# Turning all attention outputs back to features on VectorE instead of through DRAM

## The chip, the cores and the metric

One core of a Trainium2 chip runs the whole program. The metric is the time of one execution in microseconds of device time, as the median of several runs. An execution is also recorded by the hardware profiler; its span goes from the first to the last instruction, and its own time is about 2 us longer.

## The reference

Two attention blocks of width D = 640 with 32 heads of 20 features work on 2048 tokens each. Their outputs stand side by side in one result of 2048 x 1280 (bf16).

```python
# A: four segments of L = 512 tokens, causal inside a segment, plus a memory of the earlier ones
for s in range(4):
    p = softmax(qs @ ks.T * scale + causal_mask)
    a_dot = p @ vs
    a_mem = (phi(qs) @ M) / (phi(qs) @ z + 1e-6)        # phi(t) = t + 1 if t > 0 else exp(t)
    o = g * a_mem + (1 - g) * a_dot                     # g = sigmoid(beta), one per head
    M += phi(ks).T @ vs;  z += phi(ks).sum(tokens)
a = concat(o over segments, heads) @ wo_A
# B: causal attention with a window of 256 tokens
b = softmax(q @ k.T * scale + window_mask) @ v  -> heads side by side @ wo_B
out = concat([a, b], axis=-1)
```

## The kernel before

The work is cut into eight chunks of 512 tokens, alternating between the blocks: A0, B0, A1, B1, A2, B2, A3, B3, numbered n = 0 to 7. Two chunks overlap at any time, each in two halves of 16 heads. Heads are handled in eight groups g of four, one head to each 32 partitions.

For a chunk, these jobs run on the engines:

- `qk_job` (line 391) projects q and k on PE (`m` tiles, five matmuls of 128x512 each), copies them to `st`, and SP stores them to DRAM and loads them spread out (one head to 32 partitions; lines 351 and 368). `v_job` (565) projects v, and SP copies parts of it (lines 606, 618 to 621).
- `score_batch` (638) makes scores on PE into the `sc` banks of PSUM (lines 662 and 672). ACT takes their exponential into `pt` (line 682), GpSimd (POOL) masks most of them (728, 732), VectorE the half blocks (713).
- `one_group` (1270) sums p times v for a group (line 746), and for A also the memory part (`mem`, 754). The result stands as features x tokens in one PSUM bank. `turn` (763) transposes it in 32x32 blocks on VectorE into `tt` (line 769), so that tokens lie on partitions, and `norm` (773) divides by the sum (792, 787) and writes it to `o`. Where the second part of an A group comes, it is put in `u` and GpSimd adds it to `o` (804). After the turn, `o` has 32 tokens of each 32-row block on the partitions and, along the free axis, 16 blocks of tokens by 160 features of one of four head classes.
- The output projection needs features on partitions. For chunks 0 to 6, `final_job` (812) does this by DMA: four stores on SP write `o` to `scr_o` in DRAM with tokens as rows (line 818), and in `final_part` (836) a DMA transpose for each 256 tokens brings it back as `oT` (line 845), of which there are two buffers. Ten matmuls for each 128 tokens (line 857), in two halves of 320 columns, then two copies to `ot` on ACT or VectorE (lines 210 and 212), and a store to the output (870).
- For the last chunk, `back` (875) turns `o` once more on VectorE in 32x32 blocks, as soon as four groups of a 128-token tile are there, into a view of `qA`. `final_turned` (887) multiplies it with a second copy of `wo_B`, whose rows are in the order that these turns leave (`wo2`, loaded into `wk_A` by `load_wo2`, line 223).

All instructions are issued in an order that the program works out when it is built. `Flow` holds a clock for each engine, and each step adds a fixed duration to it. The main loop of `body` takes whatever is ready by those clocks: due DMAs, the next score batch, a pending group, a job, a job of `fins` (the output projections, last in the list). Work for VectorE goes in when its clock is behind PE's (`when_idle`, `flush`); where nothing is ready, PE gets a filling matmul (`fill`, line 993). The numbers of `ORDER` make small random choices between such steps at each score batch (`pick`). On the chip every engine works off its own queue strictly in order, and so does SP, which issues nearly all DMAs. There are two PSUM banks (`m0`, `m1`) for everything but scores; a bank is free again when VectorE or ACT has read it.

Of the kernel before, what the change touches and what calls it, by code (L numbers as in the profile page):

```python
# [28 lines left out]
    0, 57, 0, 852, 0, 771, 969, 354, 517, 150, 469, 627, 861, 162, 75, 0, 574, 779, 904, 517,  # L29
    524, 666, 803, 190, 0, 0, 953, 0, 405, 169, 677, 960, 622, 0, 392, 443, 517, 185, 61, 913,  # L30
    240, 994, 430, 0, 412, 385, 759, 595, 219, 521, 782, 621, 0, 804, 507, 481, 812, 481, 0,
    742, 0, 235, 388, 0, 591, 501, 847, 431, 349, 878, 434, 976, 36, 797, 549, 0, 0, 39, 668,
    959, 355, 121, 912, 0, 0, 768, 0, 679, 0, 0, 560, 924, 137, 985, 626, 0, 720, 957, 332,
    336, 390, 7, 0, 531, 661, 678, 0, 733, 400, 415, 975, 582, 0, 146, 814, 370, 94, 515, 0,
    678, 823, 209, 259, 781, 0, 814, 18, 360, 301, 230, 0, 950, 0, 406, 599, 768, 275, 0, 820,
    0, 181, 865, 0, 619, 0, 48, 579, 0, 0, 854, 0, 713, 0, 421, 775, 330, 420, 719, 898, 0,
    303, 685, 986, 0, 479, 49, 97, 362, 991, 0,
# [4 lines left out]
NOT = 2  # L42
# [133 lines left out]
class _K:  # L176
# [45 lines left out]

    def load_wo2(self, w_ap):

        self.wo2 = self.wk_A
        yield "dma", self.f.pe + 9000.0
        self.nc.sync.dma_start(out=self.wk_A[:], in_=w_ap)
        self.f.on_dma(1, 2100.0)
# [544 lines left out]
    def norm(self, tt, dst, add, last):  # L773
# [21 lines left out]
        def s2():  # L795
            if not add:
                part(dst)
                last()
                return
            u = self.wk.tile([P, NB, DH], BF16, name="u", bufs=NU)  # L800
            t = part(u[:], self.u_free[-NU])

            def both():
                nc.gpsimd.tensor_tensor(out=dst, in0=dst, in1=u[:], op=ALU.add)
                self.u_free.append(f.on_pool(716.0, t + DVE_OUT) + POOL_OUT)
                last()
            f.at(t + DVE_OUT, both)
# [4 lines left out]
    def final_job(self, n, o, scr, wo, out2d, col, t0, t1):  # L812
        nc, f = self.nc, self.f
        t = max(f.dve, f.pool) if n % 2 == 0 else f.dve
        yield "dma", t
        a, b = t0 * P, min(t1 * P, self.toks[n])
        for j in range(4):
            nc.sync.dma_start(
                out=scr[a:b, GW * j:GW * (j + 1)].rearrange("(b t) c -> t b c", t=HD),
                in_=o[HD * j:HD * (j + 1), a // HD:b // HD, :])  # L820
        t = f.on_dma(4, 1.76 * (b - a), t)
        yield "dma", t - 200.0
        for x0 in range(a, b, 256):
            yield from self.final_part(n, scr, wo, out2d, col, x0, min(b, x0 + 256), t)
        if t1 * P >= self.toks[n]:
            self.mark(f.pe, "fin", n)

# [8 lines left out]
    def final_part(self, n, scr, wo, out2d, col, a, b, t):  # L836
        nc, f = self.nc, self.f
        free = lambda: None if self.ot_n - NOT not in self.ot_done else 0.0
        while free() is None or self.urgent:
            yield "dma", free  # L840
            yield "dma", self.calm
        mine = self.ot_n
        self.ot_n += 1
        oT = self.big.tile([P, self.KT, 256], BF16, name="oT", bufs=NOT)
        nc.sync.dma_start_transpose(out=oT[:, :, 0:b - a], in_=scr[a:b, :])
        yield f.on_dma(1, 100.0, t, 950.0 + 3.83 * (b - a), 2100.0) + 600.0
        for tt in range(a // P, (b + P - 1) // P):
# [3 lines left out]
            w = min(P, b - tt * P)  # L851
            x = tt * P - a
            for hf in range(2):
                yield "bank"
                ps, bi = self.bank()
                for m in range(self.KT):
                    nc.tensor.matmul(ps[0:w, 0:320], lhsT=oT[:, m, x:x + w],  # L857
                                     rhs=wo[:, m, 320 * hf:320 * hf + 320],
# [4 lines left out]
                t = self.evac(ot[0:w, 320 * hf:320 * hf + 320], ps[0:w, 0:320], 320, 408.0)  # L863
                self.close(bi, t)
                f.open = False
            r = self.row0[n] + tt * P
            lo = max(0, -r)

            def store(ot=ot, r=r, lo=lo, w=w, k=k):
                nc.sync.dma_start(out=out2d[r + lo:r + w, col:col + self.D], in_=ot[lo:w, :])  # L870
                self.ot_free[k] = f.on_dma(1, 400.0, t + DVE_OUT)
            f.at(t + 300.0, store)
        self.ot_done.add(mine)

    def back(self, o, qt, g0):

        if g0 == 0:
            self.oD[qt] = self.qA[:].rearrange("p g s -> p (g s)")[
                :, self.D * qt:self.D * (qt + 1)].rearrange(
                "p (c b t) -> p c b t", c=LT + 1, b=LT)  # L880
        a, b = (0, 2) if g0 == 0 else (2, LT + 1)
        self.nc.vector.transpose(
            out=self.oD[qt][:, a:b, :, :].rearrange("p c b t -> p b c t"),
            in_=o[:, LT * qt:LT * qt + LT, :].rearrange("p b (c r) -> p b c r", r=HD)[:, :, a:b, :])
        self.f.on_dve(60.0 + 1.05 * P * (b - a))

    def final_turned(self, out2d, r, col, qt):
        nc, f = self.nc, self.f
        oD = self.oD[qt]
        end = qt == LT - 1  # L890
        yield f.dve + DVE_OUT
        yield from self.ot_wait()
        k = len(self.ot_free) - 1
        ot = self.wk.tile([P, 640], BF16, name="ot", bufs=3)
        for hf in range(2):
            yield "bank"
            ps, bi = self.bank()
            cs = slice(320 * hf, 320 * hf + 320)
            for m in range(self.KT):
                nc.tensor.matmul(ps[:, 0:320], lhsT=oD[:, m, :, :].rearrange("p b t -> p (b t)"),  # L900
                                 rhs=self.wo2[:, m, cs],
                                 start=(m == 0), stop=(m == self.KT - 1))
                f.on_pe("full", mm_ns(320))
                if m < self.KT - 1:
                    yield 0.0
            t = self.evac(ot[:, cs], ps[:, 0:320], 320, 408.0)
            self.close(bi, t)
            f.open = False
            if end:
                (nc.scalar if hf == 0 else nc.sync).dma_start(  # L910
                    out=out2d[r:r + P, col + 320 * hf:col + 320 * hf + 320], in_=ot[:, cs])

        def store():
            nc.sync.dma_start(out=out2d[r:r + P, col:col + self.D], in_=ot[:])
            self.ot_free[k] = f.on_dma(1, 400.0)
        if end:
            self.ot_free[k] = f.pe + 3000.0
        else:
            f.at(t + 300.0, store)
# [423 lines left out]
def laid_out(A_x, A_wq, A_wk, A_wv, A_wo, A_beta, B_x, B_wqkv, B_wo):  # L1343
# [18 lines left out]
    def heads(w):  # L1362
        return w.reshape(G, 4, DH, D).transpose(1, 0, 2, 3).reshape(D, D)
# [37 lines left out]
```

## Time and profile before

| what | us |
|---|---|
| median of 5 runs (lowest, highest) | 372.06 (369.36, 373.47) |
| time of the profiled execution | 368.91 |
| its span | 366.8 |
| TensorE matmuls busy | 331.6 |
| ScalarE busy | 318.6 |
| VectorE busy | 273.5 |
| GpSimd busy | 154.3 |

The mean granted TensorE clock was 0.986 of full speed. The DMA engines moved 61.12 MB. In the lists below, a line of a group has the source line, the engine, the operation, what it writes and reads with shapes, the count, the busy time with the mean duration of one in ns, and the idle time of the engine before it with what ended it. Busy times of groups are larger than the engine's share, as neighbours in a queue overlap by some tens of ns. A timeline line has the start, the length, the engine and line, and in square brackets the idle time before it.

### The profile page before, as it was taken

How to read it: one execution, taken by the hardware profiler on the slowest of the kernel's cores; microseconds unless marked ns; L12 is line 12 of the kernel's file. 1: busy time of each engine (PE TensorE's matmuls, PEld its weight loads, DVE VectorE, ACT ScalarE, POOL GpSimd, SP SyncE). 2: the span in 40 equal slices, each digit the busy share in tenths (PEclk: the TensorE clock that was granted, in tenths of full speed). 3: DMA queues.
4: the chain of work that ended last, by engine and by line, in shares of the span. 5: the costliest groups of instructions: out<-in, count | busy, mean ns of one | idle time of the engine just before them, and what ended most of it. 6: DMA issues, size and time to landing. Idle time of an engine off the chain costs nothing.

```text
span 366.8 us, 17742 instructions
## 1 busy us (share of the span) xinstructions
PE 331.6 (90%) x7670; PEld 185.4 (51%) x7720; DVE 273.5 (75%) x557; ACT 318.6 (87%) x412; POOL 154.3 (42%) x241
## 2 busy tenths in 40 slices
PE   8899997997989889999998699997999998997887
PEld 3445553553544544654545345553555555564554
DVE  7556884585898779988897598985888597885540
ACT  2877992997999999999999799997999899987844
POOL 8211230341345436643726365554537436365310
PEclk9999998999999999999999999997899999999999
DMA  7995574666794764567365843468333874278442
GB/s 233 410 395 149 160 169 124 166 123 179 180 278 127 157 154 125 139 179 216 118 190 157 170 112 115 128 177 205 105 117 105 216 210 124 73 154 187 121 117 100
DMA packets 85430, 61.12 MB, mean 167 GB/s; under 512 B 46056, under 2 KB 83304, under 8 KB 85352
## 3 DMA queue, kind: packets, MB, share of 16 engines
q1 hardware_dynamic: 84776, 59.57, 59.6%
q8 instruction: 60, 0.98, 1.2%
q10 hardware_dynamic: 576, 0.42, 0.4%
q14 instruction: 18, 0.15, 0.1%
HBM read 25.73 MB, written 23.72 MB: 135 GB/s over the span
## 4 chain that ended last, share of the span: by engine, by line
PE 41%; DMA 18%; ACT 16%; DVE 11%; issue 8%; SPq 4%; POOL 1%; ACTq 0%; DVEq 0%; POOLq 0%
ACT pt L682 15%; PE m L408 11%; PE m L746 7%; PE m L857 6%; PE sc L672 5%; PE m L578 4%; SPq L368 3%; PE sc L662 3%; DVE tt L769 2%; DMA pqA<-scr_pq 2%; DVE pt L713 2%; DMA wv_A<-in_A_wv_dram 2%; DMA pkT<-scr_pk 2%; DMA beta<-in_A_beta_dram 1%; DVE o L787 1%
## 5 line engine op out<-in xcount | busy, mean ns | idle before, releaser
L682 ACT ACTIVATE pt<-sc 128x1024 bf16<-128x1024 f32 (+1 forms) x328 | 283.5, 973 | 18.6 <-PE sc L672 11.8
L732 POOL TENSOR_SCALAR_AFFINE_SELECT pt<-pt 128x512 bf16<-128x512 bf16 x128 | 90.1, 704 | 161.9 <-ACT pt L682 149.1
L769 DVE STREAM_TRANSPOSE tt<-m 128x512 f32<-128x512 f32 x88 | 62.1, 711 | 30.4 <-PE m L746 28.4
L212 DVE CAST st<-m 128x512 bf16<-128x512 f32 x60 | 40.9, 681 | 16.3 <-PE m L408 13.0
L728 POOL TENSOR_SCALAR_AFFINE_SELECT pt<-pt 128x512 bf16<-128x512 bf16 x56 | 38.7, 692 | 33.4 <-ACT pt L682 33.4
L578 PEld LDWEIGHTS <-xT 128*128 128x128 bf16 x400 | 32.7, 99 | 17.3 <-issue 6.4
L787 DVE TENSOR_TENSOR o<-tt,rr 128x320 bf16<-128x320 f32 x64 | 34.7, 544 | 1.1
L857 PEld LDWEIGHTS <-oT 128*128 128x128 bf16 x280 | 24.7, 97 | 16.0 <-issue 4.6
L672 PE MATMUL sc<-qB,kB 32*128 32x64 bf16 (+3 forms) x896 | 30.2, 223 | 2.2 <-issue 1.3
L672 PE MATMUL sc<-qA,kA 32*128 32x64 bf16 (+3 forms) x640 | 29.1, 251 | 2.7 <-issue 2.0
L578 PE MATMUL m<-wv_A,xT 128*128 128x320 bf16 (+2 forms) x200 | 29.1, 285 | 2.2 <-DMA wv_A<-in_A_wv_dram 1.4
L578 PE MATMUL m<-wBv,xT 128*128 128x320 bf16 (+2 forms) x200 | 27.5, 273 | 0.7
L857 PE MATMUL m<-wo_A,oT 128*128 128x320 bf16 x160 | 26.8, 300 | 0.4 <-DVE ot L212 0.3
L408 PE MATMUL m<-xT,wBk 128*128 128x512 bf16 x83 | 24.4, 380 | 2.8 <-issue 1.4
L746 PE MATMUL m<-pt,vB 128*32 128x64 bf16 (+3 forms) x896 | 23.9, 225 | 2.7 <-ACT vB L210 1.0
L672 PEld LDWEIGHTS <-kB 32*128 32x128 bf16 x896 | 14.4, 93 | 23.2 <-issue 20.9
L408 PE MATMUL m<-xT,wBq 128*128 128x512 bf16 x89 | 24.4, 380 | 0.9 <-issue 0.3
L408 PE MATMUL m<-xT,wk_A 128*128 128x512 bf16 x78 | 22.2, 381 | 3.3 <-ACT st L210 2.2
L408 PE MATMUL m<-xT,wq_A 128*128 128x512 bf16 x82 | 23.2, 399 | 0.8 <-issue 0.2
L746 PE MATMUL m<-pt,vA 128*32 128x64 bf16 (+3 forms) x640 | 22.3, 257 | 1.4 <-ACT st L210 0.5
L857 PE MATMUL m<-wo_B,oT 128*128 128x320 bf16 x120 | 20.5, 300 | 3.2 <-ACT ot L210 1.5
L672 PEld LDWEIGHTS <-kA 32*128 32x128 bf16 x640 | 10.6, 92 | 25.4 <-issue 22.6
(99 smaller groups left out, 466.4 us busy)
## 6 DMA issues: line engine op xcount, KB each, us to landing
out_dram<-ot SPq DMA_DIRECT2D x31, 160.0 KB
scr_o<-o SPq DMA_DIRECT2D x28, 160.0 KB
scr_kB<-st SPq DMA_DIRECT2D x20, 128.0 KB
scr_qB<-st SPq DMA_DIRECT2D x20, 128.0 KB
kB<-scr_kB SPq DMA_DIRECT2D x32, 80.0 KB
qB<-scr_qB SPq DMA_DIRECT2D x32, 80.0 KB
scr_kA<-st SPq DMA_DIRECT2D x18, 128.0 KB
scr_qA<-st SPq DMA_DIRECT2D x18, 128.0 KB
```

The lines of the kernel that those rows point to most:

```text
L212: nc.vector.tensor_copy(out=out, in_=in_)
L368: self.nc.sync.dma_start(out=dst[HD * j:HD * j + DH, g0:g0 + 4, :], in_=rows.rearrange("(g j d) s -> j d g s", g=4, j=4)[j])
L408: nc.tensor.matmul(ps[:, :], lhsT=w_ap[:, kt, m * P:(m + 1) * P], rhs=xT[:, kt, :], start=(kt == 0), stop=(kt == self.KT - 1))
L578: nc.tensor.matmul(ps[:, c0:c0 + w], lhsT=xT[:, kt, tt * P:(tt + 1) * P], rhs=w_ap[:, kt, a:a + w], start=(kt == 0), stop=(kt == self.KT - 1))
L672: nc.tensor.matmul(ps[j // 2][:, j % 2, c0:c0 + 64 * nb], lhsT=k[rows, g, P * kc:P * kc + P], rhs=q[rows, g, 64 * b0:64 * (b0 + nb)], star ...
L682: nc.scalar.activation(out=pt[:, 2 * i:2 * i + 2, 0:hi], in_=ps[i][:, :, 0:hi], func=ACT.Exp, scale=self.scale)
L728: nc.gpsimd.affine_select(out=blk, in_=blk, pattern=[[0, r], [-1, w]], compare_op=ALU.is_ge, fill=self.zero, base=-1, channel_multiplier=1)
L732: nc.gpsimd.affine_select(out=blk, in_=blk, pattern=[[0, r], [1, w]], compare_op=ALU.is_ge, fill=self.zero, base=128 - w, channel_multipli ...
L746: nc.tensor.matmul(O[HD * j:HD * j + HD, c:c + 64 * nb], lhsT=self.vcols(v, h // 16 if vk[0] == "v" else 0, vt, h, HD), rhs=rhs[j], start= ...
L769: self.nc.vector.transpose(out=tt[:], in_=O[:, :])
L787: nc.vector.tensor_tensor(out=out, in0=a, in1=b, op=ALU.mult)
L857: nc.tensor.matmul(ps[0:w, 0:320], lhsT=oT[:, m, x:x + w], rhs=wo[:, m, 320 * hf:320 * hf + 320], start=(m == 0), stop=(m == self.KT - 1))
```

## The change

The way through DRAM goes for all chunks. A new job, `back_job`, is made with the first group of a chunk 0 to 6. It allocates `oD` (two buffers, 5 x 512 columns) and makes five transposes of 128x512 on VectorE, each as soon as the groups that its features come from are complete; it waits for the output projections of the chunk two before. The last chunk turns as before, in two pieces for each tile, into a buffer of `xT` in place of `qA`. Both kinds of chunk use one `final_job`, which takes `oD` as it is. `wo_A` and `wo_B` are laid out on the host in the order of rows that the turns leave, so the second copy of `wo_B` and its load go. `o` has two buffers in place of three, and a group of a chunk is only taken up once the chunk two before has been turned. Whether a part of a group is the first or is to be added is decided when its `norm` step is issued. `ORDER` has other numbers.

```diff
-    def load_wo2(self, w_ap):
...
-    def final_job(self, n, o, scr, wo, out2d, col, t0, t1):
...
-            nc.sync.dma_start(
-                out=scr[a:b, GW * j:GW * (j + 1)].rearrange("(b t) c -> t b c", t=HD),
-                in_=o[HD * j:HD * (j + 1), a // HD:b // HD, :])
...
-        nc.sync.dma_start_transpose(out=oT[:, :, 0:b - a], in_=scr[a:b, :])
...
+    def back(self, n, o, b0, nb, x, y):
+        self.nc.vector.transpose(
+            out=self.oD[n][:, x:y, b0:b0 + nb, :].rearrange("p c b t -> p b c t"),
+            in_=o[:, b0:b0 + nb, :].rearrange("p b (c r) -> p b c r", r=HD)[:, :, x:y, :])
+        self.f.on_dve(50.0 + 1.05 * HD * nb * (y - x))
+
+    def back_job(self, n, o):
+        f = self.f
+        if n >= 2:
+            yield self.known(n - 2, "out")
+        self.oD[n] = self.big.tile([P, self.KT, L // HD, HD], BF16, name="oD", bufs=2)
+        for c, last in enumerate((1, 3, 4, 6, 7)):
+            for g in range(0 if c == 0 else last, last + 1):
+                yield self.known(n, "o", g)
+            def go(c=c):
+                self.back(n, o, 0, L // HD, c, c + 1)
+                if c == self.KT - 1:
+                    self.mark(f.dve + DVE_OUT, n, "oD")
+            f.when_idle(f.pe, go, go)
+            yield f.pe + 1.0
+
+    def final_job(self, n, wo, out2d, col, qts):
...
+            yield self.known(n, "oD", qt) if n == len(self.chunks) - 1 else self.known(n, "oD")
...
-                    nc.tensor.matmul(ps[0:w, 0:320], lhsT=oT[:, m, x:x + w],
-                                     rhs=wo[:, m, 320 * hf:320 * hf + 320],
+                    nc.tensor.matmul(ps[:, 0:320], lhsT=oD[:, m, :, :].rearrange("p b t -> p (b t)"),
+                                     rhs=wo[:, m, cs],
...
-                    need = [max(p[4] for p in ps_) + 100.0, self.done.get((n, "v", g))]
+                    need = [max(p[4] for p in ps_) + 100.0, self.done.get((n, "v", g)),
+                            self.done.get((n - 2, "oD")) if n > 1 else 0.0]
...
-            o_t[n] = self.big.tile([P, L // HD, GW], BF16, name="o", bufs=3)
+            o_t[n] = self.big.tile([P, L // HD, GW], BF16, name="o", bufs=2)
+            if n < len(self.chunks) - 1:
+                self.jobs.append(self.job(self.back_job(n, o_t[n])))
+            else:
+                t = self.big.tile([P, self.KT, L], BF16, name="xT", bufs=2)
+                self.oD[n] = t[:].rearrange("p c (b t) -> p c b t", t=HD)
...
-        "A_wk": rows(A_wk), "A_wq": rows(A_wq), "A_wv": rows(A_wv), "A_wo": rows(heads(A_wo)),
+        "A_wk": rows(A_wk), "A_wq": rows(A_wq), "A_wv": rows(A_wv), "A_wo": turned(A_wo),
...
-        "B_wo": rows(heads(B_wo)), "B_wo2": turned(B_wo)}
+        "B_wo": turned(B_wo)}
```

## The prediction

> **What bounds the kernel now.** I read the page's first two parts, then the groups with shapes kept apart, the busy time of each engine in stages, and last the timelines of single engines where a stage is not full. The profiled execution took 368.91 us around a span of 366.8; the sum below is made against it. It lies 3.15 us under the median of the runs, 372.06, so the change found is then added to the median.
>
> ```profile
> PE 331.6 (90%) x7670; PEld 185.4 (51%) x7720; DVE 273.5 (75%) x557; ACT 318.6 (87%) x412; POOL 154.3 (42%) x241
> ```
>
> TensorE (PE) and ScalarE (ACT) are both nearly full, VectorE (DVE) is the third. 75% sounds like room, but it is an average. I cut the span at the half-block masks on VectorE (every third one), which stand in the same place in all queues before and after, and joined or split some stages. Columns: stretch, length, then busy time of PE, PEld, DVE, ACT, POOL.
>
> ```profile
> 116.80:143.90 27.10, 24.51 (x671) 13.10 (x676) 22.74 (x48) 25.50 (x33) 13.33 (x19) 1.00 0.59 137
> 143.90:175.00 31.10, 30.30 (x712) 17.30 (x719) 27.81 (x59) 30.92 (x39) 16.10 (x24) 1.00 0.62 177
> 175.00:206.80 31.80, 27.30 (x784) 16.27 (x782) 25.89 (x52) 30.45 (x37) 17.23 (x25) 1.00 0.61 157
> 206.80:234.80 28.00, 26.39 (x644) 13.79 (x640) 23.47 (x48) 26.80 (x33) 13.30 (x18) 1.00 0.44 119
> 330.90:347.20 16.30, 12.75 (x497) 8.15 (x496) 8.52 (x19) 12.72 (x18) 7.19 (x12) 1.00 0.68 151
> 347.20:366.85 19.65, 15.57 (x199) 10.52 (x182) 5.16 (x11) 9.09 (x19) 1.33 (x2) 1.00 0.38 113
> ```
>
> From 117 to 235 us PE is busy 92% of the time, ACT 96%, DVE 85%: no engine has much left. In the last 19.65 us no scores are made any more; PE works off output projections, and ACT and DVE are half idle or more. So the kernel ends late because output projections come late. Part of the reason is the DMA way they take, of which these lines (timelines of SP, PE and ACT) show the queue time and the waits:
>
> ```profile
> 240.33 2.00 SPq L845 DMA_TRANSPOSE oT<-scr_o  x1
> 248.24 2.29 SPq L818 DMA_DIRECT2D scr_o<-o  x4
> 325.10 2.16 SPq L845 DMA_TRANSPOSE oT<-scr_o  x1
> 338.29 0.85 PE L857 MATMUL m<-wo_B,oT 128*128 128x320 bf16 x5 [1.46 <-DMA oT<-scr_o]
> 355.85 0.76 ACT L210 CAST ot<-m 128x320 bf16<-128x320 f32 x2 [1.91 <-DMA out_dram<-ot]
> ```
>
> **What is removed.** For seven chunks: 28 stores of `o` (L818) and 14 DMA transposes (L845), and the one load of the second copy of `wo_B` into `wk_A`. Four L818 issues take 2.24 to 3.13 us of SP's queue in five places that I looked at, mean 2.65; an L845 issue has a median of 1.39. That is 7 x 2.65 + 14 x 1.39 = 38 us of SP's queue, spread over the span. SP is not counted as an engine, so this is worth only what waited behind it.
>
> **What is added.** 35 transposes of 128x512 on VectorE, five for each chunk. The last chunk already does this in two shapes:
>
> ```profile
> L882 DVE STREAM_TRANSPOSE qA<-o 128x384 bf16<-128x384 bf16 x4 | 2.3, 578 | 0.1
> L882 DVE STREAM_TRANSPOSE qA<-o 128x256 bf16<-128x256 bf16 x4 | 1.8, 445 | 0.1
> L769 DVE STREAM_TRANSPOSE tt<-m 128x512 f32<-128x512 f32 x88 | 62.1, 711 | 30.4 <-PE m L746 28.4
> ```
>
> 128 columns more cost 133 ns, so 512 cost 578 + 133 = 711 ns, the same as the f32 row of that size. 35 x 0.711 = 24.9 us. The evacuations are shared out anew as well: by counting both programs' queues, DVE does 6 fewer of `st` (681 ns), 4 more of `ot` (481), 3 fewer of `vB` and 1 more of `qA`; ACT does 4 fewer of `ot` (437) and 8 more of the large kinds. Net about +21.6 us on DVE, +2.9 on ACT. PE keeps its work: 320 output matmuls in both, 15 fills for 8, +0.8 us.
>
> (The Trainium skill, page "VectorE: DVE Perf Modes", section "The three transpose paths", gives VectorE 311 ns for 128x128 in bf16 and so speaks against this change: four such blocks are an estimated 1.24 us, 35 of them 43.5 us. Our row has 445 ns for two blocks, 222 each, so the row decides. By the page's figure 15 transposes of the filled stretch would cost 8 us more and turn the sum below into +3.)
>
> **What is moved.** Output projections start without the trip through DRAM, and the new program's order of instructions on each engine shows where they go. Matmuls of them per stage, before to after: 175 to 206.8 us, 5 to 25; 206.8 to 234.8, 0 to 46; 267.8 to 330.9, 135 to 95; after 330.9, 135 to 80. After the last score matmul 95 become 42. Now stage by stage; work is count x mean duration from the groups, and PE's is scaled by 0.93, since durations of neighbours overlap (they sum to 357 us, the engine is busy 331.6).
>
> - 14 to 117 us: PE +2.2, ACT +1.0, DVE +4.6 (8 transposes). PE is idle for 8.7 us here and DVE for 28, which hides this; SP's relief may give something. I take 0, between -3 (PE's two long gaps at 55 and 87 us, 4.6 together, mostly gone) and +3 (PE's work not hidden).
> - 117 to 175: PE +1.1, ACT +2.5, DVE +4.5 (7 transposes). ACT's idle time is 1.8 of 58.2, so +1.5; 0 to +3.
> - 175 to 235: this is the price. Durations on PE sum to 11.2 more (66 output matmuls at 139 ns are 9.2, some v products the rest), 10.4 scaled; ACT +7.0. PE was idle for 6.1 us, ACT for 2.6. At least 10.4 - 6.1 = +4.3 and 7.0 - 2.6 = +4.4; with no idle time used +10.4. The idle time before was largely waits of another kind (2 us for `pkT` at 204), which stay: +7.5.
> - 235 to 268: PE -0.4, ACT -1.0. At 249 to 261 us PE and ACT wait for `pqA` and `kA`, and the two SP lines above (2.00 and 2.29) stood ahead of their loads: -1.5, between -4 and +1.
> - 268 to 331: PE -4.6 scaled, ACT -1.3, DVE +5.2 (10 transposes, DVE idle 12 of 63). Between the two full engines: -2.5; -4.5 to +2.
> - 331 to 347: the 1.46 wait for `oT` goes, and the `vbotB` loads at 328.5 no longer stand behind a 2.16 us issue: -2, -3 to +1.
> - The end: PE's 53 fewer matmuls would be 7.4 us, but a chain takes over as the bound. Last scores at 347.2, last value product (L746) done at 351.7, turned and normalised, and the last turn back:
>
> ```profile
> 351.87 0.72 DVE L769 STREAM_TRANSPOSE tt<-m 128x512 f32<-128x512 f32 x1 [1.52 <-PE m L746]
> 353.43 0.58 DVE L882 STREAM_TRANSPOSE qA<-o 128x384 bf16<-128x384 bf16 x1
> ```
>
> It ends at 354.0; ten matmuls take 1.5; from the last output matmul to the end of the span it was 366.8 - 363.6 = 3.3 (copy, issue, store). That is 358.8 instead of 366.8: -8, between -9 and -5 (10 matmuls late). The 1.91 us wait for an `ot` buffer is inside this.
>
> Sum: 0 + 1.5 + 7.5 - 1.5 - 2.5 - 2 - 8 = **-5.0 us**. The profiled time becomes 363.9, the median 372.06 - 5.0 = **367.1 us**.
>
> New waits: `o` has two buffers instead of three and `oD` two, so the first group of a chunk waits for the turning of the chunk two before it, and that for the output projections of the one before that. Ahead of the first group of the sixth chunk the order has 20 output matmuls and then five transposes on VectorE in one row, 3.6 us. Behind them in VectorE's queue are the turns that free the two `m` banks, and PE waits for those; with about 10 us of projections and output matmuls in front and hardly a score batch, ACT runs dry there. I count this in the +7.5.
>
> **Rivals.**
> 1. *VectorE's queue becomes the bound in the filled stretch, slower.* For: DVE is 85% busy from 117 to 235 us, runs in order, and gets 15 of the transposes there, eight of them from 207 us on; PE has only two banks. Against: 18 us of DVE idle time in that stretch. If none of the 15 is hidden, 15 x 0.711 = 10.7 comes on top: -5.0 + 10.7 = +5.7, 377.8 us. From seven unhidden ones on (7 x 0.711 = 5.0) the change loses.
> 2. *Work is only moved, no change.* PE's work is the same to 0.8 us, so time changes only as PE's idle 35.2 us do. If the idle time that the new order fills is opened elsewhere by the new waits, the span is 366.8 + 0.7, the median 372.8. For: ACT was 96% busy where the work goes. Against: the end stage is a clear gain in idle ACT time (10.6 us there).
> 3. *SP's relief is worth more.* PE's gaps at 55, 87, 204 and 250 us (2.4, 2.2, 2.0, 1.8) and the clock behind two of them (granted 0.88 in 50 to 60 us, 0.66 in 250 to 260: 4.6 us of full-speed work lost) go for the better part: 7 us more, 360 us. Against: `pkT` still takes its DMA transpose, and the gap at 55 us is not a DMA wait.
>
> That the change doesn't do what it says is excluded: the new order has 35 transposes into `oD` and neither `scr_o` nor `oT`.
>
> **How the numbers follow.** Forecast (367.1) 0.32, rival 3 0.14, rival 2 0.24, rival 1 and its like 0.30. A change of about 1%, 3.7 us, is what a measurement here tells from none. Faster by over 1%: 0.32 + 0.14 = 0.46; same 0.24; slower 0.30. The range reaches from beyond rival 3 (358.5) to just over rival 1 (378.5); the forecast's own range is 362 to 371.
>
> **What would show it.** Right: DVE busy near 295 us, the new transposes near 711 ns; the stretch that was 175 to 235 longer by about 7 us; the span ending 11 to 12 us after the last score matmul instead of 19.65; no PE wait for a final's input after 330 us. Wrong: PE waits ended by VectorE's turns or copies growing by several us in the middle (rival 1); PE idle still near 35 us (rival 2); the gaps at 55 and 87 us gone (rival 3). I would be most wrong if the middle grew by more than the end gives back.

## The result, and the profile after

Nothing that can be measured. The changed kernel took 369.16 us in the median of 44 runs (364.61 to 375.25), the kernel before 370.24 us beside it (79 runs, 364.73 to 380.09); the ratio is 0.9992, 95% interval [0.997, 1.0014]. (Medians are over all runs; the ratios, here and below, are of means without the runs that lie more than 1.5% above the fastest of their kernel.) The forecast was 5.0 us less, 1.3%. The profiled execution took 365.2 us around a span of 363.5 us. That span is 3.3 us shorter than the one of before, and the first thing to read in it is the clock. The two strips below, before and then after, hold the granted TensorE clock in 40 slices of the span, where a 9 is 90% or more.

```profile
PEclk9999998999999999999999999997899999999999
```

```profile
PEclk9999999999999999999999999999999999999999
```

The profile of before has three stretches of 3.4 us at half clock, one at 58 us and two in a row from 252 to 259 us, each worth 1.7 us of full-speed work; the profile of after has none. So the pair of profiles flatters the change by about 3 x 1.7 = 5.1 us. Two stages of before hold them (columns as in the prediction, the clock stands third from the end):

```profile
50.30:85.70 35.40, 31.88 (x732) 16.57 (x733) 24.07 (x50) 27.72 (x38) 10.55 (x16) 0.95 0.60 152
234.80:267.80 33.00, 30.36 (x689) 17.02 (x692) 25.25 (x51) 30.22 (x38) 17.48 (x24) 0.90 0.61 161
```

Now the busy times of after, from its page, the group of the new transposes, and the stages that answer to those of the prediction:

```profile
PE 325.7 (90%) x7675; PEld 183.2 (50%) x7727; DVE 292.6 (81%) x588; ACT 321.2 (88%) x416; POOL 155.6 (43%) x241
```

```profile
L816 DVE STREAM_TRANSPOSE oD<-o 128x512 bf16<-128x512 bf16 x35 | 23.3, 683 | 3.0 <-PE m L854 3.0
```

```profile
116.90:146.90 30.00, 25.96 (x697) 14.11 (x691) 25.52 (x53) 25.98 (x34) 12.95 (x19) 1.00 0.46 125
146.90:178.90 32.00, 28.88 (x712) 16.69 (x705) 29.39 (x57) 31.57 (x41) 16.17 (x23) 1.00 0.55 150
178.90:210.50 31.60, 29.40 (x721) 16.93 (x717) 26.81 (x51) 31.14 (x39) 16.96 (x24) 1.00 0.57 160
210.50:249.40 38.90, 35.03 (x794) 20.56 (x798) 29.24 (x61) 34.10 (x46) 12.84 (x19) 1.00 0.42 124
338.70:352.20 13.50, 11.58 (x495) 7.77 (x494) 9.69 (x21) 11.43 (x15) 6.60 (x11) 1.00 0.19 60
352.20:363.50 11.30, 7.75 (x145) 4.97 (x130) 5.08 (x11) 4.92 (x9) 1.63 (x3) 1.00 0.22 74
```

VectorE is 19.1 us busier (21.6 were costed). The end is 11.3 us instead of 19.65. One stage pays for it: the one that took 28.00 us (206.8 to 234.8) takes 38.90. These are VectorE's and then ScalarE's timelines inside it:

```profile
236.27 3.08 DVE L816 STREAM_TRANSPOSE oD<-o 128x512 bf16<-128x512 bf16 x5 [2.98 <-PE m L854]
239.28 1.27 DVE L761 STREAM_TRANSPOSE tt<-m 128x512 f32<-128x512 f32 x2
```

```profile
228.27 1.98 ACT L674 ACTIVATE pt<-sc 128x1024 bf16<-128x1024 f32 x2
...
235.59 0.42 ACT L209 CAST ot<-m 128x320 bf16<-128x320 f32 x1 [0.25 <-PE m L854]
...
238.14 1.94 ACT L674 ACTIVATE pt<-sc 128x1024 bf16<-128x1024 f32 x2 [0.77 <-PE sc L664]
```

This is the new wait at the start of the sixth chunk: VectorE waits 2.98 us for the output projections that free an `oD` buffer, then makes all five turns of a chunk in one row, and ScalarE makes no exponential of scores from 230.25 to 238.14 us, 7.9 us. But it is not VectorE's wait that keeps the scores away, as PE's timeline shows:

```profile
226.47 0.46 PE L664 MATMUL sc<-qA,kA 32*128 32x64 bf16 x12
226.86 2.33 PE L400 MATMUL m<-xT,wBk 128*128 128x512 bf16 x9
229.03 2.32 PE L400 MATMUL m<-xT,wBq 128*128 128x512 bf16 x10
231.19 2.21 PE L570 MATMUL m<-wBv,xT 128*128 128x320 bf16 x20
...
237.65 0.40 PE L664 MATMUL sc<-qA,kA 32*128 32x64 bf16 x8
...
240.00 0.43 PE L854 MATMUL m<-wo_A,oD 128*128 128x320 bf16 x2 [1.15 <-DVE tt L761]
```

Between the score matmuls of 226.47 and 237.65 us PE's queue holds projections, output matmuls and some value products, and PE shows no wait there. Only behind the five turns does it wait, for 1.15 us. The stage is 10.9 us longer because PE is busy for 8.6 us more in it (35.03 for 26.39) and idle for 2.3 us more.

### The profile page after: what moved, and what is told of

Read it like the earlier page. It is cut to its first block, busy times and chain, and to the rows that moved or that the text cites. A ratio compares the mean times of both kernels' runs of the same rounds, so it can differ in the third digit from the quotient of the medians.

```text
span 363.5 us, 17703 instructions
## 1 busy us (share of the span) xinstructions
PE 325.7 (90%) x7675; PEld 183.2 (50%) x7727; DVE 292.6 (81%) x588; ACT 321.2 (88%) x416; POOL 155.6 (43%) x241
## 4 chain that ended last, share of the span: by engine, by line
PE 44%; DVE 20%; ACT 13%; DMA 12%; issue 8%; SPq 2%; ACTq 0%; DVEq 0%
PE m L400 15%; ACT pt L674 11%; PE m L738 7%; PE sc L664 6%; PE m L570 6%; DVE tt L761 5%; PE m L854 4%; DVE st L211 2%; DVE pt L705 2%; PE sc L654 2%; DMA qB<-scr_qB 2%; SPq L360 2%; DMA scr_qB<-st 2%; DMA wv_A<-in_A_wv_dram 2%; DVE o L779 2%
## 5 line engine op out<-in xcount | busy, mean ns | idle before, releaser
L674 ACT ACTIVATE pt<-sc 128x1024 bf16<-128x1024 f32 (+1 forms) x328 | 284.3, 973 | 19.1 <-PE sc L664 11.1
L211 DVE CAST st<-m 128x512 bf16<-128x512 f32 x54 | 36.8, 681 | 13.0 <-PE m L400 12.7
L779 DVE TENSOR_TENSOR o<-tt,rr 128x320 bf16<-128x320 f32 x64 | 37.0, 581 | 0.8
L854 PEld LDWEIGHTS <-oD 128*128 128x128 bf16 x280 | 24.8, 97 | 17.0 <-issue 7.0
L854 PE MATMUL m<-wo_A,oD 128*128 128x320 bf16 x160 | 28.0, 300 | 2.9 <-DVE tt L761 1.1
L570 PE MATMUL m<-wv_A,xT 128*128 128x320 bf16 (+2 forms) x200 | 26.8, 273 | 3.6 <-DMA wv_A<-in_A_wv_dram 2.4
L738 PE MATMUL m<-pt,vB 128*32 128x64 bf16 (+3 forms) x896 | 23.9, 225 | 4.0 <-DVE ot L211 1.0
L570 PE MATMUL m<-wBv,xT 128*128 128x320 bf16 (+2 forms) x200 | 25.7, 273 | 0.9 <-DVE tt L761 0.7
L816 DVE STREAM_TRANSPOSE oD<-o 128x512 bf16<-128x512 bf16 x35 | 23.3, 683 | 3.0 <-PE m L854 3.0
L400 PE MATMUL m<-xT,wBq 128*128 128x512 bf16 x86 | 23.9, 380 | 2.1 <-DVE tt L761 0.8
L400 PE MATMUL m<-xT,wq_A 128*128 128x512 bf16 x79 | 21.8, 380 | 2.0 <-DVE tt L761 0.8
L738 PEld LDWEIGHTS <-vB 128*32 128x32 bf16 x896 | 17.1, 96 | 12.1 <-issue 4.6
```

The lines of the kernel that those rows point to most:

```text
L211: nc.vector.tensor_copy(out=out, in_=in_)
L400: nc.tensor.matmul(ps[:, :], lhsT=w_ap[:, kt, m * P:(m + 1) * P], rhs=xT[:, kt, :], start=(kt == 0), stop=(kt == self.KT - 1))
L570: nc.tensor.matmul(ps[:, c0:c0 + w], lhsT=xT[:, kt, tt * P:(tt + 1) * P], rhs=w_ap[:, kt, a:a + w], start=(kt == 0), stop=(kt == self.KT - 1))
L674: nc.scalar.activation(out=pt[:, 2 * i:2 * i + 2, 0:hi], in_=ps[i][:, :, 0:hi], func=ACT.Exp, scale=self.scale)
L738: nc.tensor.matmul(O[HD * j:HD * j + HD, c:c + 64 * nb], lhsT=self.vcols(v, h // 16 if vk[0] == "v" else 0, vt, h, HD), rhs=rhs[j], start= ...
L779: nc.vector.tensor_tensor(out=out, in0=a, in1=b, op=ALU.mult)
```

## The experiments

Each ratio is to runs of the kernel before on the same chip, with its 95% interval. What a kernel leaves out is said in its expectation or with its edit.

**How far two groups of runs of one kernel differ.** No edit: the kernel before, once more.

> The kernel before itself, for the spread of its executions and a second profile. In 44 executions of the changed kernel the time goes with the granted clock: 365.2 us at clock 1.000, 369 to 372 at 0.986. Theory C (the clock decides between executions): the executions of before lie on one line too, about 3.7 us of time for 0.010 of clock, and a second profile at another clock has its stage lengths changed mostly where the clock was halved. Rival: time and clock of before are unrelated, and its profile at 0.986 stands for all. Ratio to before 1.000 by both.

Measured: 369.43 us, ratio 1.008 [1.0032, 1.0128]. Two groups of the same program can lie 0.8% apart, with an interval that leaves out 1. So the intervals are rather too narrow, and below I lean on differences of 1% and more only. This profile has a span of 367.5 us at a mean clock of 0.991. Without its two half-clock stretches (from 204.6 and from 310.5 us) that is 364.1 us, where the first profile of this kernel, without its three, is 361.7.

**The run time of the turns, in the changed order.** First each of the 35 turns is issued twice, then each is cut to one block of 32 columns; all else keeps its place.

```diff
-        self.nc.vector.transpose(
+        for _ in range(2 if n < 7 else 1):
+            self.nc.vector.transpose(
```

> The changed kernel with each of the 35 new transposes issued twice (same destination), the order of everything else kept: VectorE gets 24 us more work in the places where the change put it. Theory V (VectorE's queue is the price: the added transposes delay the banks that PE waits for): another 24 us costs at least as much as the first, 8 to 15 us, ratio 1.02 to 1.04. Theory S (swap: the transposes are hidden, and the output projections moved into the full middle cost there what the end gives back): under 4 us, ratio 1.00 to 1.01.

```diff
+        nw = 1 if n < 7 else nb
-            in_=o[:, b0:b0 + nb, :].rearrange(...)
+            in_=o[:, b0:b0 + nw, :].rearrange(...)
```

> The changed kernel with the 35 new transposes cut to one block of 32 columns each (128x160 features of the other tokens are left out, the rest of oD is zero), the order kept: nearly all of VectorE's added work goes, the output projections stay where they are. Theory V: the forecast gain comes out, 5 us or more, ratio 0.985 or less. Theory S: within 2 us of the changed kernel, ratio 0.995 to 1.000.

Measured: doubled 382.44 us, 1.0454 [1.037, 1.0538]; cut 365.81 us, 0.9997 [0.9957, 1.0036]. This is VectorE's timeline of the doubled kernel at the place shown above:

```profile
243.34 6.82 DVE L817 STREAM_TRANSPOSE oD<-o 128x512 bf16<-128x512 bf16 x10 [2.98 <-PE m L855]
```

Added time counts for about 70% (1.0454 less 0.9992, of 370 us, is 17 us for 23.9 us of turns). Taken away it gives little back: nothing by the ratios, 1.7 us between the profiles (both have a span of 363.5 us, but the cut one has a half-clock stretch in it), of the 17.5 us by which the 35 turns became shorter (683 to 184 ns each). PE's waits that VectorE ended, added up over the list of PE's waits, go the same way: 12.1 us in the changed kernel, 26.0 doubled, 11.7 cut. The order was planned with VectorE time set aside for the turns; most of it is not given back when they don't use it. So in this order the run time of the turns is nearly hidden, and what it costs to plan for them can't be seen in a fixed order.

**The DMA way alone.** The kernel before in its own order, without the 28 stores and 14 DMA transposes; the projections read a tile of zeros.

```diff
-            nc.sync.dma_start(out=scr[a:b, GW * j:GW * (j + 1)]..., in_=o[...])
-        nc.sync.dma_start_transpose(out=oT[:, :, 0:b - a], in_=scr[a:b, :])
+        oT = self.oTs
```

> The kernel before without the 28 stores and 14 DMA transposes of the outputs (the projections of chunks 0 to 6 read a zero tile), the order kept: shows what the way through DRAM costs the kernel before by itself. Theory D (the DMA way costs little: its waits for oT are 3 us and SP's queue has room): 2 to 4 us less, ratio 0.99 to 0.995. Rival R (SP's relief is worth more, the queue time delays q, k and v loads everywhere): 7 us or more, ratio 0.98 or less.

Measured: 359.23 us, 0.9821 [0.9759, 0.9883]. The way is worth 6.6 us. The last stage is still 18.2 us long here: the removal shortens the end by 1.45 us only. In the profile the stages that begin at 50, 86, 235 and 331 us are shorter, by 1.2, 1.6, 2.8 and 2.7 us; the first and the third of them held the half-clock stretches of before (1.7 and 3.4 us). The mean clock of its runs is 0.9975, where the runs of before beside it had 0.988: part of the gain is clock. By the slope of the last section that is 3.7 of the 9.1 us between the two means, and the other 5.4 us are 1.5%.

**The two-buffer wait and the turns, taken away one after the other.** The changed kernel, its order worked out anew: without turns for chunks 0 to 6 (projections of a tile of zeros) and with three `o` buffers; then the same with the 35 turns put back, planned, but into a scratch tile.

```diff
-            o_t[n] = self.big.tile([P, L // HD, GW], BF16, name="o", bufs=2)
-            if n < len(self.chunks) - 1:
-                self.jobs.append(self.job(self.back_job(n, o_t[n])))
+            o_t[n] = self.big.tile([P, L // HD, GW], BF16, name="o", bufs=3)
```

> The changed kernel without the buffers' waits and without the turns of chunks 0 to 6: the projections of these chunks read a zero tile and wait only for their groups, o has three buffers, no group waits for the turning two chunks before; same ORDER numbers, so the order is planned anew (22 filling matmuls on PE for 15). The kernel before without the DMA way was 0.982, the changed kernel with its turns cut 0.9997. Theory B (the two-buffer waits of o and oD bend the order: projections and turns must be done before the next chunk's groups, and scores stop meanwhile): ratio 0.980 to 0.987. Rival L (an order planned anew is worse whatever the waits; before has a lucky one): 0.995 to 1.010.

> As the run before it, but with the 35 turns of chunks 0 to 6 at full size on VectorE, written to one scratch tile that nobody reads (the projections read a zero tile); o has three buffers and waits for the turning three chunks before; 36 filling matmuls. Theory B: the turns are mostly hidden, ratio 0.982 to 0.992. Theory V (VectorE's queue): 5 to 8 us slower than the run before it, ratio 0.995 or more.

Measured: 364.01 us, 0.9824 [0.9761, 0.9886], without turns; 373.85 us, 1.0069 [1.0022, 1.0117], with. The turns cost 2.5% here (9 us), and PE's waits that VectorE ended rise from 8.3 to 13.3 us. What the first gains on the kernel before can't be read as saved work: its runs had a mean clock of 0.997, those of before beside it 0.983, and by the slope of the last section that makes 5.3 of the 5.6 us between the means. Between the two kernels (0.997 and 0.991) the clock makes 2.4 of 10.0 us. In both the long stage is short again (28.6 and 29.1 us, not 38.9), and the last stage long (17.4 and 23.4, not 11.3).

**The random choices.** `ORDER` empty, in the changed kernel and in the one before: the program then takes its first choice everywhere.

```diff
+ORDER = ()
```

> The changed kernel with ORDER empty: no random choices. The order has 99 filling matmuls on PE for 15, that is 84 x 0.109 = 9 us in which the plan finds nothing ready. Theory B (few buffers leave the plan without ready work, and ORDER has to mend that): 8 to 14 us slower, ratio 1.02 to 1.04. Rival L (orders differ by luck of a per cent or less): within 1.5%, 0.99 to 1.015.

> The kernel before with ORDER empty: 34 filling matmuls for 8, 26 x 0.109 = 2.8 us. Theory B: the structure of before needs ORDER less, 3 to 6 us slower, ratio 1.007 to 1.017, so less than the same step costs the changed kernel. Rival L: both lose the same, whatever it is.

Measured: 384.75 us, 1.0388 [1.0323, 1.0453], for the changed kernel; 376.37 us, 1.0141 [1.0069, 1.0213], for the one before. What `ORDER` does is worth 4.0% (1.0388 to 0.9992) and 1.4%: as much as any step of the change, and not the same in both. (The runs of before beside them were those at 0.983, against 0.989 and 0.992 here, so both ratios are rather too low.) From here on orders with the same search behind them are compared.

**Unplanned turns.** The kernel without turns in its own order, with the 35 turns put into VectorE's queue at once when their groups are issued, no time set aside; then the same with each issued some groups later.

```diff
+                    if cc not in turned and whole >= set(range(top + 1)):
+                        self.nc.vector.transpose(out=self.oS[:]..., in_=o[:]...)
```

> The kernel with free buffers and no turns (0.9824) with the 35 turns of chunks 0 to 6 put into VectorE's queue at full size as soon as their groups are there, without the plan knowing: every other instruction stays in its place. They write a scratch tile that nobody reads (the projections read a zero tile). Theory O (the order that is planned around turns and buffers is the price, not the turns' run time): at most 3 us more, ratio 0.982 to 0.991. Theory V (VectorE's run time, in the full middle, is the price): 6 us or more, ratio 0.998 or more.

> As the run with the turns put in without the plan (1.102, of which VectorE waited 29.9 us for GpSimd's additions), but each turn of chunks 0 to 6 stands some groups later in VectorE's queue, after the planned end of the additions it needs plus 0.9 us: run time without that wait. Scratch tile as before, projections of a zero tile, order of all else kept; without turns this order was 0.9824. Theory V (run time in VectorE's queue counts where the plan leaves no gap for it): 12 to 23 us over that, ratio 1.015 to 1.045. Theory W (the wait was all of it): 0.985 to 0.995.

Measured: at once 406.5 us, 1.102 [1.0952, 1.1089]; later 373.55 us, 1.0187 [1.0101, 1.0272]. The waits of VectorE in the first:

```profile
DVE oS L1302 <- POOL o L797: 29.9, 15, 4.5
```

Fifteen turns stand at the head of VectorE's queue for 29.9 us, waiting for GpSimd's addition into `o`, and the turns that free the two `m` banks stand behind them. Without that wait, 24.5 us of unplanned turns cost 9 to 13 us (373.55 less 364.01; 1.0187 less 0.9824, beside different runs of before). This is rival 1 of the prediction, and it is real where nothing is planned: PE's waits that VectorE ended are 44.0 us in the first, 20.6 in the second, 8.3 without turns.

**The planned turns, cut.** The kernel with 35 planned turns into scratch, in its order, each cut to one block.

```diff
+        nw = nb if n == 7 else 1
```

> The kernel with free buffers and planned turns (1.0069) with each turn of chunks 0 to 6 cut to one block of 32 columns, in the same order: the plan still keeps VectorE's time for them, the chip does not spend it. Theory O: the order alone costs what it costs, ratio 1.000 to 1.007. Theory V: most of the 9 us comes back, ratio 0.990 or less.

Measured: 370.59 us, 1.0108 [1.007, 1.0147], against 1.0069 with full turns: nothing back by the ratios, as in the changed order. So the 2.5% that the planned turns cost is not their run time.

**The same search for every kernel.** New numbers for `ORDER` in each (a search for an early planned end with the same effort in each; for the changed kernel it started from its own numbers): without turns; with planned turns into scratch; the complete changed kernel; the kernel before.

```diff
-ORDER = (0, 562, 0, 368, ...)
+ORDER = (...)                  # searched
```

> No turns of chunks 0 to 6, three buffers of o, projections of a zero tile (the kernel that gave 0.9824), with ORDER numbers from a search for the shortest plan; its plan ends at 333.6 us for 347.8 before the search. Theory P (the plan's end is what decides, so the structures differ by what they let the plan do): 8 to 14 us less than 0.9824, ratio 0.945 to 0.960. Rival L (the plan's last per cents are not the chip's): 0.975 to 0.985.

> The same with the 35 turns planned and run at full size into the scratch tile, o in three buffers, ORDER searched for with the same effort; its plan ends at 337.0, 3.4 us after the one without turns. Theory P: 3 to 5 us slower than the run without turns, ratio 0.955 to 0.970: VectorE's time can be had for little once the plan is fitted to it. Theory V: 8 us or more slower than the run without turns.

> The changed kernel itself, complete, with ORDER searched for with the same effort, from its own numbers; its plan ends at 340.4 for 344.5. Theory P: 3 to 5 us less than the changed kernel, ratio 0.985 to 0.993, and still some 4 us slower than the same with free buffers: the waits of two buffers. Rival L: 0.995 to 1.005.

> The kernel before, unchanged but for ORDER, which was searched anew with the same effort as in the three kernels with a searched order; its planned end is 335.4 us, before it was 340.6. Those three had planned ends of 333.6, 337.0 and 340.4 us and measured 0.969, 0.989 and 1.000. Theory P, the planned end tells the time whichever way the outputs take: 335.4 lies between the first two, 0.980 (363 us). Then the changed kernel at equal search effort is about 2% worse than the one before. Theory D, the DMA way costs on the chip what the plan does not count for it (its removal alone was worth 1.8% in a fixed order): the shorter plan is not kept, 0.995 to 1.005.

| kernel, searched | planned end, us | ratio, interval | long stage, us | last stage, us |
|---|---|---|---|---|
| no turns, three `o` | 333.6 | 0.9687 [0.9587, 0.9786] | 28.1 | 13.3 |
| planned turns to scratch, three `o` | 337.0 | 0.9888 [0.9827, 0.9949] | 31.8 | 14.8 |
| complete changed kernel | 340.4 | 1.0000 [0.9957, 1.0043] | 39.1 | 11.8 |
| kernel before | 335.4 | 0.9985 [0.994, 1.0031] | 27.4 | 18.7 |

More search gives neither complete kernel anything (their planned ends fell by 4.1 and 5.2 us, to 340.4 and 335.4): the tie is not one of unequal tuning. The planned turns cost 2.0% again (2.6% by the means of all runs, 356.2 and 365.5 us); 0.9687 is more than one of its expectations and less than the other. The kernel before has an earlier planned end than the one with planned turns and is 1% slower by the ratios, 0.2% by the means of all runs; that the DMA way costs on the chip what the plan does not count would fit this, but it is not shown by it. A short end need not go with a long stage: the kernel without turns has 28.1 and 13.3 us. The wait for the two buffers is +1.1% here (0.9888 to 1.0000; 0.7% by the means of all runs), while in the first pair it was -0.8% (1.0069 to 0.9992, where the former was planned with the latter's numbers of `ORDER`): its sign is not settled.

**The DMA way out only at the end.** The kernel before with chunks 5 and 6, then only 6, turned on VectorE (128x640 at a time, into the buffers that the DMA transposes filled; three `o` buffers stay), searched alike. And the changed kernel with turns for 128 tokens at a time into four small buffers, so that `o` keeps three, searched too.

```diff
+        if n in VEC:                       # (5, 6), then (6,)
+            nc.vector.transpose(out=oT[:, :, P * i:P * i + P]..., in_=o[...]...)
+        else:
             nc.sync.dma_start_transpose(out=oT[:, :, 0:b - a], in_=scr[a:b, :])
```

> The kernel before, with chunks 5 and 6 turned on VectorE (each 256 tokens into the same two buffers that the DMA transposes fill) and chunks 0 to 4 left on the DMA way; both second copies of the output weights are loaded late; o keeps three buffers; ORDER searched with the same effort, planned end 335.2 us. Theory P: the same as the kernel before with a searched order, 0.980 each, within 0.5%. Theory D: the part of the DMA way that stands in the last 100 us goes, where the chip showed waits for it, so it beats the kernel before with a searched order by 0.5 to 1.5%.

> As the one with chunks 5 and 6 turned on VectorE, but only chunk 6, whose projections stand in the last 40 us; planned end 334.2 us. Theory P: 0.974. Theory D: between the kernel before with a searched order and the one with two chunks turned, 0.985 to 0.995.

> The changed kernel, with all turns of a chunk made per tile of 128 tokens (640 columns, 28 turns in place of 35) once all groups of the chunk are there, into four small tiles of oD in turn, so that o keeps three buffers in the same memory; ORDER searched, planned end 341.1 us. Theory P: 1.002 (370 us). If the coupling of two o buffers with two oD buffers is what costs the last 1.1%, and the plan misjudges it, this one comes out near the kernel with planned turns and free buffers, 0.989.

Measured: two chunks 364.61 us, 0.9929 [0.9882, 0.9976]; one chunk 365.02 us, 0.9957 [0.9911, 1.0002]; small buffers 380.72 us, 1.0386 [1.0314, 1.0458], far from both of its expectations. The first has the lowest ratio of all complete kernels here, 0.7% under the kernel before, but by the first experiment that is no safe gain. Its eight turns are cheap, and it keeps the stages short (27.7 the long one, 17.2 the last):

```profile
L860 DVE STREAM_TRANSPOSE oT<-o 128x640 bf16<-128x640 bf16 x8 | 6.3, 816 | 0.9 <-PE m L881 0.9
```

The small buffers lose 3.9% against the changed kernel's searched order, nearly all in the long stage (51.9 us for 39.1). Timelines of ScalarE and SP there:

```profile
252.40 0.43 ACT L210 CAST ot<-m 128x320 bf16<-128x320 f32 x1 [7.01 <-DMA out_dram<-ot]
255.08 1.94 ACT L675 ACTIVATE pt<-sc 128x1024 bf16<-128x1024 f32 x2 [2.25 <-PE sc L665]
```

```profile
243.34 1.44 SPq L361 DMA_DIRECT2D qB<-scr_qB  x4
244.88 2.25 SPq L317 DMA_DIRECT2D xT<-in_B_x_dram  x5
247.17 1.51 SPq L361 DMA_DIRECT2D pqA<-scr_pq  x4
248.78 4.53 SPq L874 DMA_DIRECT2D out_dram<-ot  x4
```

Projections that stand close together need their three `ot` buffers back; the stores that free them stand behind three groups of loads on SP, and ScalarE and VectorE (6.61 us) wait with their queues full. The single wait by `oD` was replaced by a worse one by `ot`.

## Why the prediction was wrong

Stage by stage, forecast, then after less before as profiled, then with the half-clock stretches of before taken out (1.7 us in the first row, 3.4 in the fourth). The stages begin where the matmuls of half-block scores start on PE (L662 before, L654 after); the prediction named their masks on VectorE, which come some us later.

| stage of before, us | forecast | profiles | at full clock |
|---|---|---|---|
| 0 to 117 | 0 | +0.1 | +1.8 |
| 117 to 175 | +1.5 | +3.8 | +3.8 |
| 175 to 235 | +7.5 | +10.7 | +10.7 |
| 235 to 268 | -1.5 | -4.3 | -0.9 |
| 268 to 331 | -2.5 | -2.5 | -2.5 |
| 331 to 347 | -2 | -2.8 | -2.8 |
| the end | -8 | -8.35 | -8.35 |
| sum | -5.0 | -3.35 | +1.75 |

The last column stands on one profile of before. Its repeat is 364.1 us at full clock, and against that one the changed kernel's 363.5 are 0.6 us less. So the balance is near nothing and its sign is not settled, as the medians (-1.1 us) say. The rise from 117 to 235 us is not in doubt: 14.5 us against the first profile, 14.1 against the second.

- **The step that failed** is the overlap in the filled stretch. The terms for 117 to 175 and 175 to 235 us were taken as +1.5 and +7.5, 9.0 together; the stages grew by 14.5. The bounds there were +3 and +10.4, and both were passed (3.8 and 10.7). The work itself was counted well: 11.5 us more on PE were forecast (1.1 and 10.4), 10.8 came (119.3 busy for 108.5). But the sum let part of this work hide in idle time, and none of it did: PE's idle time in the stretch rose from 9.5 to 13.2 us. PE's waits that VectorE ended rose there from 1.3 to 5.5 us by the list of PE's waits; those ended by all else went from 6.2 to 5.7. Four lines of these lists, over the whole span, show the same wait of projections for a turn into `tt`, which frees a bank, two of before and then two of after (in all, times, longest):

```profile
PE m L408 <- DVE tt L769: 0.3, 2, 0.2
PE m L857 <- DVE tt L769: 0.2, 1, 0.2
PE m L400 <- DVE tt L761: 1.8, 5, 0.8
PE m L854 <- DVE tt L761: 1.3, 2, 1.1
```

  Of the rise, 1.15 us stand behind the five turns in one row. The new wait for an `oD` buffer, 2.98 us, was foreseen; it holds up VectorE and not PE. The run time of the turns is the smaller part: with the turns cut to a block the stretch is still 131.4 us long (133.1 less one half-clock stretch, for 132.5), though PE's waits for VectorE in it fall to 3.2 us. Which feature of the new order makes the rest stays open.
- **The baseline.** The sum was made against one profile that ran at 0.986, and only rival 3 named the slow clock; the sum did not take it out, neither of the first term nor of that for 235 to 268 us. The two half-clock stretches of that stage were no debt of the DMA way alone: other executions of the same program have theirs elsewhere, as the last section shows. At full clock the stage gained 0.9, not 4.3.
- **What was right**: 35 turns at 683 ns for the 711 taken, VectorE at 292.6 for "near 295"; the end at 11.3 for "11 to 12"; no wait for `oT`; the place and the form of the new wait. The gaps at 55 and 87 us, whose end was to speak for rival 3, are gone (the longest of PE in 50 to 95 us is 1.06), but the first row of the table shows that nothing came of it. The Trainium skill's page "VectorE: DVE Perf Modes", section "The three transpose paths", has 311 ns for 128x128; the runs have 683 to 712 ns for four such blocks, 816 for five, far less for each.
- **The shorter end is real, but it is no gain.** Without the DMA way and with nothing else changed the last stage is 18.2 us. What shortens it are the output projections that the new order makes earlier, before 250 us. Long stage and last stage together: before 47.65 us, after 50.2, without the DMA way 46.5. The work came back with 2.55 us on top.
- **The rivals.** Rival 2, work only moved, is the nearest: its +0.7 us stands against -1.1 us in the medians, and its sign came: PE is idle for 37.8 us, after 35.2. Rival 1's sign came too, PE's waits for VectorE growing in the middle (1.3 to 5.5 us). Over the whole span the listed waits of PE that VectorE ended rose from 5.7 to 12.1 us and all others fell from 22.6 to 17.0 (7.9 and 20.5 in the repeat of before): a relief and a price that cancel. The experiments give rough sizes. The removal of the DMA way alone saves 1.5 to 1.8%, the kind of saving that rival 3 named, and planned turns cost 2.0 to 2.5% in two pairs. That price is not rival 1's unhidden run time, since turns cut to a block gave next to nothing back. Two pairs are few where `ORDER` alone moves a kernel by 1.4 to 4.0%, so a lucky or unlucky order may be part of these sizes. How much of the balance is the wait for two buffers stays open.

## What to carry to other kernels

Work that is moved into a stretch where the engines are nearly full should be booked in full, unless one can name the idle time that it will use. When an order is planned by a program, an operation's price can be what the plan must set aside for it and not its duration: test it by planning with and without it, with the same search on both sides, and not only by cutting it from a fixed order. A gain at the end of a program that comes from work made earlier is to be booked together with the stage that the work goes to. Before two profiles are subtracted, bring both to the same granted clock, and take a second profile of one: here two of the same kernel lay 2.4 us apart even then.

## What the runs showed of the hardware

- **Time follows the granted clock from run to run.** Over 195 runs of 19 kernels, each taken about its kernel's mean, time falls with the clock with a correlation of -0.84 and 379 us for the whole clock. One half-clock stretch of 3.4 us is 0.0046 of the mean clock, so 1.75 us by this slope, against 1.7 by its length. Most of the spread of one kernel goes with the clock, and so with how many such stretches an execution catches (the square of the correlation is 0.70): the runs of the changed kernel go from 365.2 us at 1.000 to 372.8 and more at 0.977 to 0.982.
- **The same gap of PE brings one in one execution and none in the next.** These are two gaps of the repeat of the kernel before (PE's timeline):

```profile
58.23 0.29 PE L529 MATMUL m<-vA,pkT 128*32 128x64 bf16 x14 [2.07 <-issue]
...
204.99 1.46 PE L529 MATMUL m<-vA,pkT 128*32 128x64 bf16 x96 [2.15 <-DMA pkT<-scr_pk]
```

  Behind the first the clock stays full, where the first profile of the same kernel has a half-clock stretch behind the same gap (2.36 us); behind the second it falls (0.58 over 204 to 208 us), where the first profile has none. The Trainium skill's page "TensorE: Matmul & The Clock Gate", section "Part 1: The HAM clock gate (the "warmup" mystery)", has a free-running window of about 3.4 us, after which an idle array goes to half rate. The length agrees, and where a gap falls in such windows could explain the difference, which no run here shows; but here gaps of 2.15 and 2.36 us, shorter than a window, were enough, and the two stretches in a row of the first profile begin behind waits of 0.46 and 0.90 us.
- **A turn at the head of VectorE's queue that waits for GpSimd costs more than its length**: 24.9 us of turns and 29.9 us of waits made the kernel 12% slower than the one without them (1.102 less 0.9824, some 44 us), and the mean clock of its runs was 0.948.
